# Down products of three groups one pair of Gate and Up later, cuts of w2 further apart, and a cast marked urgent

## The chip, the cores and the metric

The kernel runs on one core of a Trainium2 chip. The metric is the device time of one execution in microseconds (us). The core has TensorE (PE, matmuls), VectorE (DVE), ScalarE (ACT), GpSimd (POOL) and SyncE (SP, which issues the transfers). Each engine works through its own instructions in order and waits by semaphores for the others. Matmul results land in PSUM banks, which VectorE and ScalarE read and so set free.

## The reference

For x of 2048 tokens by 512, the kernel computes a block with windowed attention (32 heads of 16, each token sees itself and the 255 before it) that is multiplied by a gate from a SwiGLU network:

```python
xn = _layernorm(x, axis=-1)
s = _A_ref(xn, A_wqkv, A_wo)              # softmax attention in a window of 256, then @ wo
g = _silu(_B_ref(xn, B_w1, B_w3, B_w2))   # silu(silu(xn @ w1) * (xn @ w3)) @ w2, 1792 wide inside
return x + s * g
```

All inputs and the output are float32.

## The kernel before

**Precision.** Each float32 operand is held as a pair of float16 parts, a high and a low one. A product takes three matmuls: high by high, high by low and low by high. Before a weight block is cut into parts it is scaled by a factor worked out from sums of its squares. For the first tokens this is done inside the kernel: ScalarE squares the block and adds up (L249 for w1 and w3, L941 for w2), VectorE casts the sums (L261, L945), TensorE multiplies them with ones (L285), and a chain of small VectorE steps (L294 to L304, L956 to L966) makes the scale. The cut is then `split_pool` (ACT L342 and L343, POOL L345), for the first group of w2 `split` (ACT L333, DVE L334). The cut blocks are also stored in DRAM, from where the later tokens load them.

**Tiles and stages.** The tokens are worked in four tiles t of 512. The hidden width of 1792 is cut into 14 blocks f of 128 (0 to 13). For each block, `gate_up` computes Gate (12 matmuls in two halves, L1058) and then Up (12, the same line). Gate's bank is read by Tanh on ScalarE (L1073) and by a product on VectorE (L1077); Up's by a product on VectorE (L1082). A cast on ScalarE (L1091) and a subtraction on GpSimd make the pair for Down. `down(t, k, b)` (L1283) sums the blocks of group k, GROUPS = (0,4), (4,8), (8,11), (11,14), into 128 tokens b of 0 to 3, and VectorE adds each sum to an accumulator (L1304 for the first group, L1307 for the others). "Block 5" below is Gate and Up of f = 5.

**Banks.** Gate, Up, Down, `project` (Q and K, L601, read by ACT L618 and DVE L622) and the values (L567) share two banks, m0 and m1: each dense piece takes the other one, so a piece waits until the piece before the last has been read out. Scores use two buffers `s` and one `po`.

**The order.** `feed_forward` makes one list of dense pieces for the whole network. Attention is cut into units, and `spread` puts five batches of each unit (scores by column L759, masked on DVE L766 and exponentiated on ACT L769; scores by row L671, whose maxima VectorE takes at L685; values L787) between those pieces. Each piece that costs anything is a step; `later(n, f)` runs f n steps on. TensorE's instructions stay in the order in which the program writes them; those of the other engines are ordered by a scheduler by priority, and `with urgent()` gives high priority. Some of the steps, loads and measures among them, are tied to the places of the Gate and Up pieces in the list. A piece that is made early may issue its transfer, and everything that hangs on it, earlier.

`late` is what follows a pair of Gate and Up. In before, when the last block of a group has been listed, the four Down products of that group are put into `late`, and so they come after the Gate and Up of the next block: group 0 behind block 4, group 1 behind block 8, group 2 behind block 11.

Of the kernel before, what the change touches and what calls it, by code (L numbers as in the profile page):

```python
# [34 lines left out]
FB = F // P  # L35
# [48 lines left out]
def tile_block(ctx: ExitStack, tc: tile.TileContext, x, wqkv, wo, w1, w3, w2, out):  # L84
    nc = tc.nc
# [52 lines left out]
    def urgent():  # L138


        return tc.high_priority(offset=200) if started else nullcontext()
    made_so_far = [0]

    def later(n, f):
        made_so_far[0] += 1
        queue.append((now[0] + n, made_so_far[0], f))
# [776 lines left out]
    NORMS = {}  # L923
# [9 lines left out]
    def measure_down(k, f):  # L933

        f0, f1 = GROUPS[k]
        n = f1 - f0
        if f == f0:
            NORMS[k] = small.tile([P, n], F32, name="ssq2")
        sq = ppool.tile([P, D], BF16, name="sqa", bufs=1)
        with behind_exp():  # L940
            nc.scalar.activation(sq, RAW2[f], AF.Square, accum_out=NORMS[k][:, f - f0:f - f0 + 1])  # L941
        if f < f1 - 1:
            return
        sb = small.tile([P, n], BF16, name="sb2")
        nc.vector.tensor_copy(sb, NORMS[k])  # L945

        def scale(s):
            p2 = small.tile([P, n], F32, name="pp2")
            def bound():
                with tc.issue_after(lasts["emptied"].ins):  # L950
                    rest(p2)
            return then(s, powers(sb, n, p2, None, s), lambda: later(1, bound))

        def rest(p2):
            assert measured >= set(range(f0, f1))
            nc.vector.tensor_mul(p2, p2, p13[:, f0:f1])  # L956
            q = small.tile([P, 1], F32, name="q")
            nc.vector.tensor_reduce(q, p2, axis=AX.X, op=ALU.max)
            nc.vector.tensor_scalar(down_scale[:, k:k + 1], q, 1.0 / (HS * WS), None, op0=ALU.mult)
            if k:  # L960
                nc.vector.tensor_max(fold_q, fold_q, q)
            else:
                nc.vector.tensor_copy(fold_q, q)
            nc.vector.reciprocal(q, q)
            sw = small.tile([P, 4], F32, name="sw2")
            nc.vector.tensor_scalar(sw[:, 0:n], p13[:, f0:f1], q, WS, op0=ALU.mult, op1=ALU.mult)  # L966

            def cut(f):
                raw = RAW2.pop(f)
                WF.setdefault((0, f), [[None, None], None])[1] = b = take(F16)  # L970
                if k == 0:
                    with tc.issue_after(lasts["emptied"].ins):
                        split(b[:, 0:D], b[:, D:], raw, sw[:, f - f0:f - f0 + 1])
                else:
                    with behind_exp():
                        split_pool(b[:, 0:D], b[:, D:], raw, sw[:, f - f0:f - f0 + 1])
                give(raw, after=5)
            for i, f in enumerate(range(f0, f1)):
                later(1 + 2 * i, lambda f=f: cut(f))
            if f1 == FB:  # L980
                later(4, fold_scales)
        beside_scores(2, scale)
# [288 lines left out]
    def down(t, k, b):  # L1271

        f0, f1 = GROUPS[k]
        cell = {}

        def part(fs):
            if fs[0] == f0:
                cell["ps"] = bank([P, D])
            ps = cell["ps"]
            for f in fs:  # L1280
                hh, w = HH[t, f], WF[t, f][1]
                for i, (a, c) in enumerate(((0, 0), (0, 1), (1, 0))):
                    nc.tensor.matmul(ps, hh[:, a * TW + b * P:a * TW + (b + 1) * P], w[:, c * D:(c + 1) * D],  # L1283
                                     start=f == f0 and i == 0, stop=f == f1 - 1 and i == 2)
                if b == 3:
                    give(hh)
                    if t == 0:
                        def store(f=f, w=w):
                            nc.sync.dma_start(dW2[f], w)
                            give(w, after=3)  # L1290
                        later(4, store)
                    else:
                        give(w)
            if fs[-1] < f1 - 1:
                return
            if k == len(GROUPS) - 1:
                summed.add((t, b))
            if k == 0:
                ACC[t, b] = take(F32)
                with urgent():  # L1300
                    if t:
                        nc.scalar.activation(ACC[t, b], ps, AF.Copy, scale=down_scale[:, 0:1])
                    else:
                        lasts["emptied"] = nc.vector.tensor_scalar(ACC[t, b], ps, down_scale[:, 0:1], None, op0=ALU.mult)  # L1304
            else:
                with urgent():
                    lasts["emptied"] = nc.vector.scalar_tensor_tensor(ACC[t, b], ps, down_scale[:, k:k + 1], ACC[t, b],  # L1307
                                                                      op0=ALU.mult, op1=ALU.add)
        return opening([(3 * len(fs), lambda fs=fs: part(fs)) for fs in (range(f0, f0 + 2), range(f0 + 2, f1))])
# [67 lines left out]
    def feed_forward():  # L1377

        pieces = []
        late = []  # L1380
        cuts_at = []
        for t in range(NT):
            for f in range(FB):
                if t == 0:

                    if (f % 2 or f == 0) and f + LEAD < FB - 2:
                        pieces += [(0, lambda f=f: load(0, f)) for f in (range(f + LEAD, f + LEAD + 2) if f else range(4, LEAD + 1))]
                    elif f + LEAD == FB - 1:
                        pieces += [(0, lambda f=f: load(0, f)) for f in range(FB - 2, FB)]
                    if f % 2 and f + 3 < FB:  # L1390
                        pieces.append((0, lambda f=f + 3: later(8, lambda: measure(f, 1, 6)) if f == 6 else measure(f, 1)))
                    pieces += [(0, lambda f=f: load_down(0, f)) for f in range(f + 2 if f else 0, min(f + 3, FB))]
                    for m in range(f + 1 if f else 0, min(f + 2, FB)):
                        k = next(k for k, (_, f1) in enumerate(GROUPS) if m < f1)
                        pieces.append((0, lambda k=k, m=m: later(2, lambda: measure_down(k, m))))
                else:
                    if f == 0:
                        pieces += [(0, lambda t=t, f=f: load(t, f)) for f in range(2)]
                    if f + 2 < FB:
                        pieces.append((0, lambda t=t, f=f + 2: load(t, f)))  # L1400

                    if t == 1:
                        pieces.append((0, lambda t=t, f=f: load_down(t, f)))
                    if t == 1 and f in FOLD_AT:
                        work = fold_weights(FOLD_AT.index(f))
                        pieces.append((0, work[0]))
                        cuts_at.append((f + 2, work))
                    for at, work in cuts_at:
                        if t == 1 and f == at:
                            pieces.append((0, work[1]))  # L1410
                if f == FB - 4 and t + 2 < NT:
                    first, second = prepare_beside(t + 2, 8)
                    pieces += first
                if f == 0 and t > 2:
                    pieces += soon
                made = gate_up(t, f)
                for at, work in cuts_at:
                    if t == 1 and f == at:
                        made.insert(2, (0, lambda work=work: later(6, work[2])))
                pieces += made  # L1420
                pieces += late
                late = []
                if t < 2:
                    for k, (f0, f1) in enumerate(GROUPS):
                        if f == f1 - 1:
                            late = [q for b in range(4) for q in down(t, k, b)]
                for k, (j0, j1) in enumerate(FOLDS):
                    if t > 1 and f == 2 * j1 - 1:
                        soon, late = folds(t, k)
                        if k == 0 or t == NT - 1:  # L1430
                            pieces += soon
            if t + 2 < NT:
                pieces.append((0, second))
        return pieces + late
# [193 lines left out]
    for n in range(len(units)):  # L1628
        t = n // 8
# [8 lines left out]
        b = n % 8 - (2 if t < 3 else 3)  # L1638
# [6 lines left out]
    for n, u in enumerate(units):  # L1645
# [17 lines left out]
        k = n // 2 + 2  # L1663
# [35 lines left out]
```

## Time and profile before

| | |
|---|---|
| median of 3 runs | 805.73 us (805.66 to 805.86) |
| the profiled execution | 805.44 us |
| its span | 803.7 us |
| mean granted clock of TensorE | 0.999 |
| instructions in the span | 23972 |
| VectorE busy | 624.2 us (78%) |
| ScalarE busy | 393.0 us (49%) |

The span runs from the first to the last instruction that the profile shows; the execution's own time has 1.74 us more around it. In timelines the columns are start, duration, engine, source line, operation, output and inputs, shapes, the number of instructions that the row holds, and in brackets the idle time before it with what ended it. A line's number in the profile of before is one lower than in the changed kernel from L946 on, since one line was added there, and five lower from the end of `feed_forward` on. Matmuls overlap: one with 512 columns lasts 380 ns in a row, but starts come 216 ns apart in an undisturbed run of them.

### The profile page before, as it was taken

How to read it: one execution, taken by the hardware profiler on the slowest of the kernel's cores; microseconds unless marked ns; L12 is line 12 of the kernel's file. 1: busy time of each engine (PE TensorE's matmuls, PEld its weight loads, DVE VectorE, ACT ScalarE, POOL GpSimd, SP SyncE). 2: the span in 40 equal slices, each digit the busy share in tenths (PEclk: the TensorE clock that was granted, in tenths of full speed). 3: DMA queues.
4: the chain of work that ended last, by engine and by line, in shares of the span. 5: the costliest groups of instructions: out<-in, count | busy, mean ns of one | idle time of the engine just before them, and what ended most of it. 6: DMA issues, size and time to landing. Idle time of an engine off the chain costs nothing.

```text
span 803.7 us, 23972 instructions
## 1 busy us (share of the span) xinstructions
PE 791.4 (98%) x9181; PEld 404.3 (50%) x9181; DVE 624.2 (78%) x2005; ACT 393.0 (49%) x592; POOL 382.1 (48%) x746
## 2 busy tenths in 40 slices
PE   8999999999999999999999999999999999999997
PEld 4444444444554444444445444466544754466465
DVE  8887887888898678887888888777768876874537
ACT  6988685754455544345343344344444234444411
POOL 2355467552429445365443546330446276650770
PEclk9999999999999999999999999999999999999999
DMA  9887654836665564667555733665463553334431
GB/s 283 238 261 239 187 179 117 286 98 205 188 214 188 158 221 131 216 153 250 137 195 157 226 119 102 167 177 162 132 164 85 160 155 112 89 114 136 128 97 53
DMA packets 109858, 134.18 MB, mean 167 GB/s; under 512 B 18928, under 2 KB 64944, under 8 KB 109744
## 3 DMA queue, kind: packets, MB, share of 16 engines
q1 hardware_dynamic: 109456, 132.13, 55.3%
q8 instruction: 72, 1.18, 0.6%
q10 hardware_dynamic: 288, 0.52, 0.2%
q14 instruction: 42, 0.34, 0.1%
HBM read 91.23 MB, written 36.57 MB: 159 GB/s over the span
## 4 chain that ended last, share of the span: by engine, by line
PE 82%; DVE 6%; ACT 4%; DMA 3%; issue 2%; SPq 1%; POOL 0%; DVEq 0%; ACTq 0%; POOLq 0%
PE m L1058 30%; PE po L787 9%; PE m L601 9%; PE m L1283 8%; PE m L1201 7%; PE s L759 5%; PE m L1335 4%; PE m L567 4%; PE s L671 3%; PE po L671 2%; DVE junk L685 2%; ACT pt L769 1%; DMA dW<-slot 1%; ACT slot L342 1%; DVE s L766 1%
## 5 line engine op out<-in xcount | busy, mean ns | idle before, releaser
L1058 PE MATMUL m<-XH,slot 128*128 128x512 f16 x896 | 267.3, 380 | 1.2 <-DVE slot L622 0.8
L769 ACT ACTIVATE pt<-s,es 128x1024 f32<-128x1024 f32 x152 | 167.6, 1112 | 184.4 <-DVE s L766 180.4
L1058 PEld LDWEIGHTS <-slot 128*128 128x128 f16 x1344 | 125.0, 98 | 155.1 <-issue 12.5
L1058 PE MATMUL m<-XL,slot 128*128 128x512 f16 x448 | 169.8, 379 | 0.0
L766 DVE TENSOR_TENSOR s<-s,MK 128x256 f32<-128x256 f32 (+2 forms) x280 | 118.9, 435 | 53.6 <-PE s L759 48.2
L685 DVE CUSTOM_DVE_ANT_0 junk<-s,MW 128x320 bf16<-128x320 f32 x276 | 134.1, 486 | 18.7 <-PE s L671 10.6
L339 POOL TENSOR_TENSOR slot<-slot,slot 128x256 f16<-128x256 f32 (+1 forms) x86 | 57.6, 693 | 119.5 <-DVE slot L1339 54.3
L345 POOL TENSOR_TENSOR slot<-slot,slot 128x128 f16<-128x128 f32 x168 | 68.6, 442 | 73.5 <-ACT slot L343 68.2
L685 DVE CUSTOM_DVE_ANT_0 junk<-po,MW 128x320 bf16<-128x320 f32 x172 | 83.5, 486 | 5.3 <-DVE M L685 0.5
L1283 PE MATMUL m<-slot,slot 128*128 128x512 f16 x336 | 78.5, 380 | 0.3 <-DVE slot L1077 0.2
L787 PE MATMUL po<-pt,V 64*32 64x320 f32 (+4 forms) x2880 | 77.2, 342 | 0.8 <-DVE XL L525 0.8
L601 PE MATMUL m<-XH,slot 128*128 128x512 f16 x240 | 70.8, 380 | 0.4 <-DVE slot L1077 0.4
L1201 PE MATMUL m<-slot,slot 128*128 128x256 f16 x588 | 68.4, 273 | 0.1
L1073 ACT ACTIVATE slot<-m,sgs 128x512 f32<-128x512 f32 x56 | 38.3, 684 | 54.7 <-PE m L1058 54.1
L1116 POOL TENSOR_TENSOR slot<-slot,slot 128x256 f16<-128x256 f32 x98 | 64.5, 670 | 1.1
L787 PEld LDWEIGHTS po<-pt,V 64*32 64x32 f32 x2880 | 50.7, 106 | 22.6 <-PE s L515 0.9
L1201 PEld LDWEIGHTS <-slot 128*128 128x128 f16 x588 | 56.2, 98 | 11.6 <-issue 3.0
L1077 DVE SCALAR_TENSOR_TENSOR slot<-slot,m 128x512 f32<-128x512 f32 x56 | 38.3, 684 | 27.4 <-ACT slot L1073 27.4
L759 PE MATMUL s<-qa,KA 50*64 50x320 f16 (+3 forms) x1472 | 58.3, 259 | 0.1
L601 PEld LDWEIGHTS <-slot 128*128 128x128 f16 x392 | 36.5, 98 | 42.5 <-issue 1.9
L759 PEld LDWEIGHTS <-KA 50*64 50x64 f16 x1472 | 30.1, 105 | 51.9 <-issue 32.2
L1283 PEld LDWEIGHTS <-slot 128*128 128x128 f16 x336 | 30.7, 98 | 38.7 <-issue 4.3
(191 smaller groups left out, 1134.7 us busy)
## 6 DMA issues: line engine op xcount, KB each, us to landing
slot<-dW SPq DMA_DIRECT2D x98, 256.0 KB
slot<-in_B_w_dram SPq DMA_DIRECT2D x56, 256.0 KB
slot<-dFold SPq DMA_DIRECT2D x48, 256.0 KB
dW<-slot SPq DMA_DIRECT2D x42, 256.0 KB
slot<-in_A_x_dram SPq DMA_DIRECT2D x30, 256.0 KB
KA<-dK SPq DMA_DIRECT2D x24, 288.0 KB
slot<-dWQ SPq DMA_DIRECT2D x24, 256.0 KB
qa<-dQ SPq DMA_DIRECT2D x30, 192.0 KB
```

What stands on the lines that cost most here:

```text
L339: op(out[:, c], a[:, c], b[:, c])
L345: nc.gpsimd.tensor_sub(lo[:, c:c + P], raw[:, c:c + P], hi[:, c:c + P])
L601: nc.tensor.matmul(cell["pp"][:, cols[n]], w[:, (a * NC + c) * P:(a * NC + c + 1) * P], b[:, c, cols[n]], start=n == 0 and (c, i) == parts ...
L685: lasts["maximum"] = nc.vector.tensor_tensor_reduce(out=junk[:, :n], in0=s[:, r, :n], in1=mask, scale=1.0, scalar=NEG, op0=ALU.add, op1=AL ...
L759: nc.tensor.matmul(s[64 * h:64 * h + 64, r, o:o + 64 * n], ka[rows, 2 * p + a, 64 * (m + 4):64 * (m + 5)], qa[rows, 2 * p + a, 64 * (m + k ...
L766: nc.vector.tensor_add(v, v, MK[:, kind, of:of + n, :].unsqueeze(1).to_broadcast([P, 2 * len(which), n, 64]))
L769: lasts["exp"] = nc.scalar.activation(pt, s, AF.Exp, scale=es)
L787: nc.tensor.matmul(cell["po"][32 * i:32 * i + 32, h, 64 * (m + k):64 * (m + k + n)], V[64 * h:64 * h + 64, (4 * t + m // 2) % VB, hd * VW: ...
L1058: nc.tensor.matmul(cell[k], w[:, (a * NC + c) * P:(a * NC + c + 1) * P], b[:, c, :], start=c == 0 and i == 0, stop=c == NC - 1 and i == 2)
L1116: nc.gpsimd.tensor_sub(lo, view, hi)
L1201: nc.tensor.matmul(cell["ps"][:, c], made[:, f:f + P], wj[:, g:g + 256], start=j == j0 and c == 0 and n == 0, stop=j == j1 - 1 and n == 2, ...
L1283: nc.tensor.matmul(ps, hh[:, a * TW + b * P:a * TW + (b + 1) * P], w[:, c * D:(c + 1) * D], start=f == f0 and i == 0, stop=f == f1 - 1 and ...
```

## The change

Three edits. The cast of w2's summed squares is marked urgent. The cuts of w2's blocks come four steps apart instead of two, for all groups but the last. And for the first 512 tokens the Down products of groups 0 to 2 pass through a second list, `next_late`, so that they come after the Gate and Up of one more block: group 0 behind block 5, group 1 behind block 9, group 2 behind block 12. The number of instructions on each engine stays the same.

```diff
@@ measure_down
         sb = small.tile([P, n], BF16, name="sb2")
-        nc.vector.tensor_copy(sb, NORMS[k])
+        with urgent():
+            nc.vector.tensor_copy(sb, NORMS[k])
...
             for i, f in enumerate(range(f0, f1)):
-                later(1 + 2 * i, lambda f=f: cut(f))
+                later(1 + (4 if f1 < FB else 2) * i, lambda f=f: cut(f))
@@ feed_forward
-        late = []
+        late, next_late = [], []
...
                 pieces += made
                 pieces += late
-                late = []
+                late, next_late = next_late, []
                 if t < 2:
                     for k, (f0, f1) in enumerate(GROUPS):
                         if f == f1 - 1:
-                            late = [q for b in range(4) for q in down(t, k, b)]
+                            products = [q for b in range(4) for q in down(t, k, b)]
+                            if t == 0 and f1 < FB:
+                                next_late = products
+                            else:
+                                late = late + products
```

The next pieces show the order of instructions on an engine, before and after. First TensorE, where Up 4 ends (m1_1317 before, m1_1314 after is its bank). Before:

```order
L1058 LDWEIGHTS slot26_1089
L1058 MATMUL m1_1317<-XH_301,slot26_1089 128x512
L1058 LDWEIGHTS slot26_1089
L1058 MATMUL m1_1317<-XL_302,slot26_1089 128x512
L1283 LDWEIGHTS slot46_788
```

And after, at the same place:

```order
L1059 LDWEIGHTS slot26_1089
L1059 MATMUL m1_1314<-XH_301,slot26_1089 128x512
L1059 LDWEIGHTS slot26_1089
L1059 MATMUL m1_1314<-XL_302,slot26_1089 128x512
L1059 LDWEIGHTS slot17_1152
L1059 MATMUL m0_1349<-XH_301,slot17_1152 128x512
```

Gate 5 (m0_1349) stands where Down of group 0 stood. The Down products come 80 rows later, after Up 5 (m1_1415):

```order
L1059 LDWEIGHTS slot14_1188
L1059 MATMUL m1_1415<-XH_301,slot14_1188 128x512
L1059 LDWEIGHTS slot14_1188
L1059 MATMUL m1_1415<-XL_302,slot14_1188 128x512
L1284 LDWEIGHTS slot46_788
L1284 MATMUL m0_1439<-slot15_1196,slot46_788 128x512
```

Down (m0_1439) stands directly behind Up 5, in the bank that Gate 5 took.

VectorE at the same time. `po_1304` and `po_1301` are the same scores by row, slot19_1270 and slot18_1267 are Up 4's result. Before:

```order
L334 SCALAR_TENSOR_TENSOR slot45_1325<-slot51_807,sw2_1178,slot45_1325 128x512
L685 ISA junk_1302,M_1111<-s_1295,M1_106 128x256
L685 ISA M_1111 128x1
L685 ISA junk_1309,M_1111<-po_1304,MW_111 128x320
L685 ISA M_1111 128x1
L1082 SCALAR_TENSOR_TENSOR slot19_1270<-m1_1317,slot19_1270 128x512
L685 ISA junk_1311,M_1111<-po_1304,MW_111 128x320
L685 ISA M_1111 128x1
L766 TENSOR_TENSOR s_1354<-s_1354,MK_119 128x4x64
```

After:

```order
L685 ISA junk_1299,M_1111<-s_1292,M1_106 128x256
L685 ISA M_1111 128x1
L685 ISA junk_1306,M_1111<-po_1301,MW_111 128x320
L685 ISA M_1111 128x1
L685 ISA junk_1308,M_1111<-po_1301,MW_111 128x320
L685 ISA M_1111 128x1
L1083 SCALAR_TENSOR_TENSOR slot18_1267<-m1_1314,slot18_1267 128x512
L334 SCALAR_TENSOR_TENSOR slot21_1357<-slot42_711,sw2_1178,slot21_1357 128x512
L261 CAST sb_1270<-ssq_1269 128x4
L766 TENSOR_TENSOR s_1365<-s_1365,MK_119 128x4x64
```

The cut of w2 (L334) and Up's product stand behind the maxima of `po` instead of ahead of them, and a cast of sums of w1 and w3 (L261) has come in ahead of the mask addition.

ScalarE between Tanh 7 and the read-out of the project (L618, the last row of each piece). Before, thirteen instructions stand between them; these are the last eleven, and L618:

```order
L249 ACTIVATE sqa_2010,ssq_1928<-slot38_1569 128x512
L343 CAST slot24_1995<-slot8_1007 128x512
L769 ACTIVATE pt_2043<-s_2030,es1_396 128x1024
L249 ACTIVATE sqa_2020,ssq_1928<-slot0_1573 128x512
L342 ACTIVATE slot13_1107<-slot13_1107,sw2_1979 128x512
L342 ACTIVATE slot29_1103<-slot29_1103,pi_1771 128x512
L343 CAST slot4_2022<-slot13_1107 128x512
L769 ACTIVATE pt_2126<-s_2113,es1_396 128x1024
L343 CAST slot11_2071<-slot29_1103 128x512
L342 ACTIVATE slot18_1254<-slot18_1254,sw2_1979 128x512
L1091 CAST slot32_2085<-slot46_2008 128x512
L618 ACTIVATE slot34_2181<-m1_2105 128x512
```

After, Tanh 7 (L1074) and all that stands between:

```order
L1074 ACTIVATE slot25_2022<-m1_1997,sgs_155 128x512
L342 ACTIVATE slot8_1007<-slot8_1007,sw2_1993 128x512
L249 ACTIVATE sqa_2034,ssq_1949<-slot31_1342 128x512
L343 CAST slot14_2009<-slot8_1007 128x512
L769 ACTIVATE pt_2050<-s_2037,es1_396 128x1024
L342 ACTIVATE slot13_1107<-slot13_1107,sw2_1993 128x512
L1092 CAST slot3_2085<-slot25_2022 128x512
L343 CAST slot47_2087<-slot13_1107 128x512
L769 ACTIVATE pt_2128<-s_2115,es1_396 128x1024
L941 ACTIVATE sqa_2170,ssq2_2006<-slot51_1951 128x512
L249 ACTIVATE sqa_2321,ssq_2309<-slot46_2097 128x512
L618 ACTIVATE slot32_2178<-m1_2107 128x512
```

Ten instructions stand between instead of thirteen: the cuts of blocks 8 and 9 (pi_1771) are done earlier in the program, and squares of later blocks have come in.

## The prediction

> **What bounds the kernel now.** I read the page's busy times first, then the table of stretches, then TensorE's timeline in the stretches that show idle time, and last the timelines of ScalarE and VectorE at those places.
>
> The page's span and its busy times (busy, share of the span, instructions):
>
> ```profile
> span 803.7 us, 23972 instructions
> PE 791.4 (98%) x9181; PEld 404.3 (50%) x9181; DVE 624.2 (78%) x2005; ACT 393.0 (49%) x592; POOL 382.1 (48%) x746
> ```
>
> TensorE is busy for 791.4 of 803.7 us, so the time is TensorE's work plus its holes, 12.3 us. The stretches (busy time of each engine, granted clock, DMA share) show where the holes lie:
>
> ```profile
> core 0: us, PE busy (x) PEld busy (x) DVE busy (x) ACT busy (x) POOL busy (x), PEclk, DMA share, GB/s
> 60.00:100.00 40.00, 38.55 (x354) 17.62 (x352) 32.30 (x118) 29.93 (x56) 18.63 (x43) 1.00 0.69 213
> 100.00:140.00 40.00, 36.99 (x528) 19.04 (x527) 32.80 (x124) 28.26 (x53) 28.14 (x72) 1.00 0.47 147
> 140.00:200.00 60.00, 60.00 (x646) 28.18 (x644) 51.26 (x188) 35.06 (x56) 25.31 (x65) 1.00 0.61 194
> 200.00:760.00 560.00, 559.08 (x6943) 287.50 (x6942) 432.61 (x1336) 243.70 (x319) 270.47 (x473) 1.00 0.54 159
> ```
>
> The order changes only between about 70 us (the end of Up 4) and about 200 us; before and after that TensorE has the same instructions in the same order. In this stretch it idles 1.45 + 3.01 = 4.46 us, all of it before 140 us. From 140 to 760 us there is 0.92 us of idle time. So a gain or loss made before 140 us is carried to the end whole: nothing behind it waits long enough to swallow it. The most that the change can win is about 4.4 us.
>
> The instructions are the same in number and kind in both kernels, so every term is a wait that grows or goes. I compare the start of a fixed TensorE instruction in before with where it must come after. Each hole is named by the row behind it; the brackets hold the idle time and its releaser.
>
> **At block 5.** TensorE's rows where Down of group 0 now stands (start, duration, instruction):
>
> ```profile
> 70.69 1.46 PE L1283 MATMUL m<-slot,slot 128*128 128x512 f16 x6 [0.25 <-DVE slot L1077]
> 72.24 0.42 PE L759 MATMUL s<-qa,KA 50*64 50x320 f16 x10
> 73.08 0.33 PE L671 MATMUL s<-KA,qa 48*64 48x320 f16 x4 [0.43 <-ACT pt L769]
> 73.89 0.33 PE L671 MATMUL po<-KA,qa 48*64 48x320 f16 x4 [0.47 <-DVE M L685]
> 74.15 5.35 PE L1283 MATMUL m<-slot,slot 128*128 128x512 f16 x24
> 79.44 0.33 PE L671 MATMUL s<-KA,qa 48*64 48x320 f16 x4
> 79.60 0.18 PE L285 MATMUL s<-sb,onesb 64*64 64x4 bf16 x4
> ```
>
> ScalarE, VectorE and GpSimd there, from their own timelines:
>
> ```profile
> 69.22 0.70 ACT L1073 ACTIVATE slot<-m,sgs 128x512 f32<-128x512 f32 x1
> 76.19 1.09 ACT L769 ACTIVATE pt<-s,es 128x1024 f32<-128x1024 f32 x1
> 69.94 0.69 DVE L1077 SCALAR_TENSOR_TENSOR slot<-slot,m 128x512 f32<-128x512 f32 x1 [0.41 <-ACT slot L1073]
> 71.09 0.75 DVE L334 SCALAR_TENSOR_TENSOR slot<-slot,sw,slot 128x512 f16<-128x512 f32 x1
> 66.05 1.94 POOL L345 TENSOR_TENSOR slot<-slot,slot 128x128 f16<-128x128 f32 x4 [0.17 <-ACT slot L343]
> ```
>
> In the row at 70.69 Down starts right behind Up 4 and waits until Gate 4's bank is emptied: Tanh at 69.22, product at 69.94, free at 70.63. After the change Gate 5 stands in that place and takes the same bank, so this wait stays. The exponential for which 73.08 waits has the same instructions ahead of it in both orders: no change. The wait of 73.89 is for the maxima that empty `po`. One cut of w2 (L334, 0.75 us) and the Up product (L1082) stand ahead of them on VectorE. After the change the cut comes later and the maxima stand ahead of both, so this wait goes: 73.89 comes right behind 73.08, as 0.16 us lie between the rows 79.44 and 79.60. I take 0.65 us of gain for the 0.81 between 73.08 and 73.89.
>
> What is new is the wait behind it. Gate 5 then ends at 74.8 and Up 5 (12 matmuls at 5.35 / 24 = 0.22 us each, from the row of 74.15: 2.6 us) at 77.4. Down's first matmul needs Gate 5's bank. Tanh 5 stands on ScalarE right behind the exponential that runs from 76.19 to 77.2 in before. So: Tanh 77.2, product 0.72 later (69.22 to 69.94) at 77.9, bank free 0.69 later, at 78.6. TensorE waits from 77.4 to 78.65, 1.25 us. The sum at the row of 79.44 is −0.65 + 1.25 = **+0.60**. The bounds of that hole: about 0 if the exponential in front of Tanh 5 runs a whole length (1.09) earlier than in before, and 2.3 (1.25 + 1.09) if it runs as much later. I keep 1.25: on ScalarE the instructions ahead of that exponential are of the same kinds as in before, and its row is there.
>
> The weights of block 5 don't hold Gate 5 back: the last of their cuts on GpSimd ends at 68.0 (66.05 + 1.94), 2.7 us ahead.
>
> **From 87 to 101 us.** TensorE again, and the cast that the urgent mark moves:
>
> ```profile
> 87.79 0.30 PE L671 MATMUL po<-KA,qa 48*64 48x256 f16 x4
> 88.02 0.61 PE L1058 MATMUL m<-XH,slot 128*128 128x512 f16 x2
> 95.73 0.31 PE L671 MATMUL po<-KA,qa 48*64 48x320 f16 x4
> 96.24 0.59 PE L1058 MATMUL m<-XH,slot 128*128 128x512 f16 x2 [0.20 <-DVE slot L622]
> 100.22 0.33 PE L671 MATMUL s<-KA,qa 48*64 48x320 f16 x4
> 100.88 0.20 PE L285 MATMUL s<-sb,onesb 64*64 64x4 bf16 x4 [0.33 <-DVE sb L945]
> 100.66 0.17 DVE L945 CAST sb<-ssq 128x4 bf16<-128x4 f32 x1
> ```
>
> At 96.24 Gate 6 waits for the project's bank (L622). After the change the project stands further ahead and Down's bank, emptied by one VectorE instruction, is taken: 95.73 to 96.24 is 0.51, the same step without a wait (87.79 to 88.02) 0.23, so **−0.28**. At 100.88 the product with ones waits for the cast of the sums, which VectorE does at 100.66 although the sums were long complete. In before the cast stands on VectorE directly ahead of the product of Gate 6, after the change ten instructions stand between them: 0.66 between 100.22 and 100.88, 0.16 without a wait, so **−0.50**. By 101 us the net is −0.18, say −0.2.
>
> **From 105 to 126 us.** TensorE, then ScalarE:
>
> ```profile
> 111.23 0.59 PE L601 MATMUL m<-XH,slot 128*128 128x512 f16 x2 [0.43 <-DVE slot L1077]
> 113.76 0.30 PE L671 MATMUL s<-KA,qa 48*64 48x256 f16 x4 [0.73 <-ACT pt L769]
> 119.98 0.59 PE L1058 MATMUL m<-XH,slot 128*128 128x512 f16 x2 [0.43 <-DVE slot L622]
> 122.35 0.38 PE L1058 MATMUL m<-XL,slot 128*128 128x512 f16 x1
> 122.81 1.46 PE L1283 MATMUL m<-slot,slot 128*128 128x512 f16 x6
> 124.48 0.33 PE L671 MATMUL s<-KA,qa 48*64 48x320 f16 x4 [0.22 <-DVE al L295]
> 125.83 1.58 PE L787 MATMUL po<-pt,V 64*32 64x320 f32 x49 [0.79 <-DVE XL L525]
> 109.78 0.67 ACT L1073 ACTIVATE slot<-m,sgs 128x512 f32<-128x512 f32 x1
> 110.35 0.61 ACT L343 CAST slot<-slot 128x512 f16<-128x512 f32 x1
> 112.60 1.11 ACT L769 ACTIVATE pt<-s,es 128x1024 f32<-128x1024 f32 x1
> 118.60 0.60 ACT L618 ACTIVATE slot<-m 128x512 f16<-128x512 f32 x1
> 121.34 0.69 ACT L1073 ACTIVATE slot<-m,sgs 128x512 f32<-128x512 f32 x1
> ```
>
> At 111.23 the project waits for Gate 7's bank. Tanh 7 (109.78) stands behind the same number of instructions in both kernels, and ScalarE is not late because of TensorE there; TensorE arriving 0.2 earlier waits 0.2 longer. The net returns to **0**, with ±0.2.
>
> Then ScalarE's queue is shorter, since the cuts of blocks 8 and 9 were done earlier. Between Tanh 7 and the exponential at 112.60 stand three instructions instead of four; one cast takes 110.35 to 110.86, some 0.5 us. So the hole of 0.73 at 113.76 shrinks by at most 0.5; I take **−0.40**. Between Tanh 7 and the project's L618 (118.60) stand ten instead of thirteen, so L618 may run 1.5 us earlier; the wait of 0.43 at 119.98 goes, with the gap in the pipeline 0.84 to 0.36: **−0.48**. Tanh 8 (121.34) follows earlier, and with it the bank that 122.81 waits for: 0.46 from 122.35, against one interval of 0.22, is **−0.24**. On VectorE the mask add, the steps of the scale chain (L295) and the split of the transposed scores (L525) stand behind the product of Gate 8. With that product earlier the step to 124.48 loses its idle 0.22 and a little of the pipeline's fill: **−0.28**; of the idle 0.79 at 125.83 I take half, **−0.42**, since the transposition in front still has to be done.
>
> **The sum.** 0 + (−0.40 − 0.48 − 0.24 − 0.28 − 0.42) = **−1.8 us**. After 126 us Gate 9 and Up 9 stand where the second group's Down stood. Scores and values lie between Gate 9 and the moved Down, and a project between Gate 12 and the third group's Down, so Tanh has over 3.5 us there, and I count nothing. The profiled execution took 805.44 us, its span 803.7; the sum gives a span of 801.9, an execution of 803.6. It lies 0.29 under the median of 805.73, so the median becomes **803.9 us**. A measurement of this kernel can tell about 0.2% from no change, 1.6 us, so the forecast is just beyond it.
>
> **Rivals.** *The later gains don't come (wash), 805.4 us.* ScalarE's queue is shorter, but if score blocks arrive as late as before (the mask adds on VectorE set the exponential), L618 and Tanh 8 stay where they are. Then 0 to −0.4 is left, 805.3 to 805.7. For it: VectorE is busy 32.80 of 40 us in 100 to 140. Against it: the rows at 113.76 and 119.98 wait on ScalarE's instructions. Chance 0.27.
>
> *No hole at block 5, 802.6 us.* If ScalarE does Tanh 5 early enough, the hole of 1.25 is gone, and TensorE keeps that lead if Tanh 7 comes earlier with it; −1.8 − 1.25 = −3.1. Chance 0.09.
>
> *The bank wait takes over (slower), 807.9 us.* Down's first matmul comes right behind Up, and at block 5 only Up's 2.6 us covers Tanh and product, at block 9 Up and the scores before it, 3.6 (72.24 to 73.08 and the four products behind, 0.84 + 0.16). If the product ends more than 4.9 us behind its Gate's last matmul (the forecast has 3.8), the hole at block 5 is 2.3, and at block 9 it is 1.3. The sum: −0.65 + 2.3 − 0.28 − 0.50 + 1.3 = +2.2, provided that the later start of everything on TensorE also delays VectorE's and ScalarE's chain, so that 111 us resets nothing and the gains of 113 to 126 are void. It decides from the one exponential more or less that stands ahead of Tanh 5. Chance 0.15.
>
> *The clock drops.* More short waits at banks could let the clock fall. Two rows of short stretches at the start show its price:
>
> ```profile
> 1.00:4.00 3.00, 2.96 (x8) 1.07 (x9) 1.83 (x4) 2.34 (x2) 2.96 (x15) 1.00 0.65 227
> 4.00:8.00 4.00, 3.80 (x18) 1.64 (x17) 3.47 (x12) 2.74 (x4) 1.30 (x4) 1.00 1.08 329
> ```
>
> In the first, matmuls come 0.375 us apart (3.00 / 8), in the second 0.222 (4.00 / 18). A slow stretch of 3 us costs 3.00 − 8 × 0.222 = 1.2 us; two of them, one at block 5 and one at block 9, take 2.4 from the 1.8 gained: +0.6, 806.3 us. Against it: the longest hole in before, 0.79, slowed nothing behind it, and the row at 74.15 with 24 matmuls holds full pace straight after two holes. Chance 0.02. The Trainium skill ("TensorE: Matmul & The Clock Gate", section "A second HAM failure mode: psum-queue depth-cycling") states that a kernel which cycles through PSUM banks can idle so briefly and often that the clock gate swings between half and full, and that the cost lies in the re-warming and not in the single matmul. That rule speaks against this change, which adds such a wait; the row at 74.15 does not agree with it here.
>
> That the change does nothing isn't a rival: the order shows the moves.
>
> **How the numbers follow.** The forecast has 0.47, spread over 802.9 to 804.9: of it I put 0.39 beyond −0.2% and 0.08 within. The wash gives 0.24 within and 0.03 faster, the case without a hole 0.09 faster, the bank wait 0.15 slower, the clock 0.02 within, since 806.3 is inside 0.2%. Faster 0.39 + 0.03 + 0.09 = 0.51, same 0.08 + 0.24 + 0.02 = 0.34, slower 0.15. The range reaches down to 802.4, past most of the case without a hole, and up to 806.8, past the wash and short of the bank wait's 807.9: some 0.04 below and 0.16 above are left out.
>
> **What would show it right or wrong.** In the profile of the changed kernel, Down's first matmul behind Up 5 has an idle of about 1.1 us released by the product; the product with ones of w2's sums has none by the cast; the projects' and Gates' rows between 113 and 126 have 1.8 us less idle in sum; from 140 us on there is none. It is wrong if a hole of over 0.5 us stands at block 9 or 12, if idle between 100 and 140 stays at 3.0, or if matmuls of 128x512 come more than 0.22 us apart anywhere behind 8 us.

## The result and the profile after

The changed kernel takes 803.86 us (median of 15 runs, 803.48 to 804.58), the kernel before 805.73 us in the same comparison. The ratio is 0.9979, with a 95% interval of 0.9971 to 0.9986: 1.9 us or 0.21% faster, between 0.14% and 0.29%. One of the 15 executions of before took 826.34 us and is not in the ratio. The forecast was 803.9 us.

The table of stretches of the changed kernel (busy time of each engine, granted clock, DMA share); its span is 801.8 us:

```profile
60.00:100.00 40.00, 38.06 (x354) 17.26 (x352) 33.08 (x124) 34.19 (x66) 23.25 (x55) 1.00 0.69 217
100.00:140.00 40.00, 39.12 (x517) 19.62 (x516) 35.57 (x136) 29.84 (x55) 25.79 (x66) 1.00 0.53 164
140.00:200.00 60.00, 59.69 (x665) 28.41 (x663) 49.20 (x177) 32.98 (x50) 27.38 (x73) 1.00 0.58 188
```

TensorE's idle time from 60 to 100 us grew from 1.45 to 1.94 us, from 100 to 140 it fell from 3.01 to 0.88, and from 140 to 200 it is 0.31 where there was none. ScalarE is busy for 34.19 instead of 29.93 us in the first stretch and for 29.84 instead of 28.26 in the second: work of both stretches has moved forward, and squares of later blocks have come into the second. The clock is 1.00 in all of them, so that rival did not come.

TensorE's timeline at the places of the prediction (start, duration, instruction, and in brackets the idle time with its releaser), in the changed kernel:

```profile
70.69 0.59 PE L1059 MATMUL m<-XH,slot 128*128 128x512 f16 x2 [0.25 <-DVE slot L1078]
73.09 0.33 PE L671 MATMUL s<-KA,qa 48*64 48x320 f16 x4 [0.60 <-ACT pt L769]
73.22 0.33 PE L671 MATMUL po<-KA,qa 48*64 48x320 f16 x4
78.64 1.46 PE L1284 MATMUL m<-slot,slot 128*128 128x512 f16 x6 [1.09 <-DVE slot L1078]
80.02 0.33 PE L671 MATMUL s<-KA,qa 48*64 48x320 f16 x4
96.53 0.60 PE L1059 MATMUL m<-XH,slot 128*128 128x512 f16 x2
100.68 0.18 PE L285 MATMUL s<-sb,onesb 64*64 64x4 bf16 x4
111.04 0.59 PE L601 MATMUL m<-XH,slot 128*128 128x512 f16 x2 [0.47 <-DVE slot L1078]
113.12 0.30 PE L671 MATMUL s<-KA,qa 48*64 48x256 f16 x4 [0.28 <-ACT pt L769]
118.68 0.33 PE L671 MATMUL po<-KA,qa 48*64 48x320 f16 x4
119.18 0.60 PE L1059 MATMUL m<-XH,slot 128*128 128x512 f16 x2
121.78 0.59 PE L1059 MATMUL m<-XH,slot 128*128 128x512 f16 x2
123.17 0.33 PE L671 MATMUL s<-KA,qa 48*64 48x320 f16 x4
123.66 2.06 PE L787 MATMUL po<-pt,V 64*32 64x320 f32 x72
146.40 0.59 PE L1059 MATMUL m<-XH,slot 128*128 128x512 f16 x2 [0.19 <-DVE slot L1308]
```

And ScalarE and VectorE around Tanh 5, the project's read-out and Tanh 8:

```profile
76.19 1.09 ACT L769 ACTIVATE pt<-s,es 128x1024 f32<-128x1024 f32 x1
77.19 0.68 ACT L1074 ACTIVATE slot<-m,sgs 128x512 f32<-128x512 f32 x1
117.00 0.58 ACT L618 ACTIVATE slot<-m 128x512 f16<-128x512 f32 x1
118.79 0.68 ACT L1074 ACTIVATE slot<-m,sgs 128x512 f32<-128x512 f32 x1
77.90 0.69 DVE L1078 SCALAR_TENSOR_TENSOR slot<-slot,m 128x512 f32<-128x512 f32 x1 [0.78 <-ACT slot L1074]
```

The reader sees the chain at block 5 as it was worked out: exponential 76.19, Tanh 77.19, product 77.90, Down at 78.64. The read-out of the project (L618) runs at 117.00 instead of 118.60, Tanh 8 at 118.79 instead of 121.34. Of the ten rows with a marked wait that the prediction showed between 70 and 126 us, three start where they did or nearly so and still wait (70.69, 73.09, 111.04), one has a shorter wait (113.12), the other six waits are gone; 78.64 and 146.40 are new. At 118.68 and at 188.57 no wait is marked, but there are small ones of 0.13 and 0.12 us, of which more below.

Start against start (the changed kernel less before, at the same instruction or the same place in the order), with the forecast beside it:

| row in before | forecast, sum so far | measured |
|---|---|---|
| 79.44, scores behind Down or Up | +0.60 | +0.58 |
| 96.24, Gate 6 | +0.32 | +0.29 |
| 100.88, product with ones | −0.18 | −0.20 |
| 111.23, project | 0 ± 0.2 | −0.19 |
| 113.76, scores by row | −0.40 | −0.64 |
| 119.98, Up 8 | −0.88 | −0.80 |
| 122.81, Down before, Gate 9 after | −1.12 | −1.03 |
| 124.48, scores by row | −1.40 | −1.31 |
| 125.83, values | −1.82 | −2.17 |
| end of the span | −1.8 | −1.9 |

### The profile page after: what moved, and what is told of

Same layout as the page of the kernel before. It is cut to its first block, busy times and chain, and to the rows that moved or that the text cites. A ratio compares the mean times of both kernels' runs of the same rounds, so it can differ in the third digit from the quotient of the medians.

```text
span 801.8 us, 23974 instructions
## 1 busy us (share of the span) xinstructions
PE 791.1 (99%) x9181; PEld 403.8 (50%) x9181; DVE 623.0 (78%) x2005; ACT 393.9 (49%) x592; POOL 381.2 (48%) x746
## 4 chain that ended last, share of the span: by engine, by line
PE 80%; DVE 8%; DMA 4%; ACT 3%; issue 2%; POOL 1%; SPq 1%; DVEq 0%; ACTq 0%; POOLq 0%
PE m L1059 31%; PE po L787 9%; PE m L601 8%; PE m L1202 8%; PE m L1284 7%; PE s L759 5%; PE m L1336 4%; PE m L567 4%; PE s L671 3%; DMA slot<-in_B_w_dram 2%; DVE junk L685 2%; PE po L671 2%; ACT sqa L249 1%; DVE s L766 1%; POOL slot L345 1%
## 5 line engine op out<-in xcount | busy, mean ns | idle before, releaser
L787 PE MATMUL po<-pt,V 64*32 64x320 f32 (+4 forms) x2880 | 77.2, 342 | 0.1
L1074 ACT ACTIVATE slot<-m,sgs 128x512 f32<-128x512 f32 x56 | 38.3, 684 | 59.8 <-PE m L1059 59.7
```

Of the source, the lines that this page charges most:

```text
L787: nc.tensor.matmul(cell["po"][32 * i:32 * i + 32, h, 64 * (m + k):64 * (m + k + n)], V[64 * h:64 * h + 64, (4 * t + m // 2) % VB, hd * VW: ...
```

## Experiments

The start of the row at block 5 (70.69 in both kernels) differs between profiled executions by up to 0.6 us, although the instructions ahead of it are the same. So starts are compared less that start. The first table column is the median with that of before in the same comparison; "project" is the row of 111 us, "scores" that of 113 us, "last" the start of the last matmul of the execution.

| kernel | median, before | start at block 5 | project | scores | last |
|---|---|---|---|---|---|
| before | 805.73 | 70.69 | 40.54 | 43.07 | 728.8 |
| changed | 803.86, 805.73 | 70.69 | 40.35 | 42.43 | 727.0 |
| e1, cast alone | 805.93, 805.81 | 70.91 | 40.61 | 43.15 | 729.1 |
| e2, delay alone | 804.99, 805.81 | 70.85 | 40.35 | 43.06 | 728.7 |
| e3, no cast | 804.50, 805.81 | 71.23 | 40.39 | 42.48 | 727.3 |
| e4, no spacing | 805.13, 805.81 | 71.16 | 40.37 | 43.08 | 728.1 |
| e5, group 0 | 803.11, 805.85 | 70.85 | 40.36 | 42.45 | 726.0 |
| e6, groups 1 and 2 | 806.35, 805.85 | 71.08 | 40.61 | 43.15 | 729.3 |
| e7, larger hole | 804.89, 805.85 | 71.04 | 40.87 | 42.96 | 727.6 |
| e8, rstd early | 804.48, 805.85 | 70.64 | 40.68 | 42.77 | 728.4 |
| e9, smaller hole | 803.03, 805.99 | 71.22 | 39.95 | 42.03 | 725.6 |
| e10, groups 0 and 1 | 804.31, 805.99 | 71.27 | 40.36 | 42.46 | 726.7 |
| e11, group 0, no cast | 803.41, 805.99 | 70.75 | 40.36 | 42.45 | 726.1 |

The profiled execution of e2 took 805.63 us, 0.6 above its median, with a wait of 0.53 at 522 us in it, so its last column is late. The traces of e2, e4 and e7 each have a wait of about 0.25 us at 710 to 711 us, and no other trace has it; their last column holds it too. The intervals of the ratios are some 1.5 us wide, and most of the changed kernels differ by less, so what separates two of them is read from the traces.

### e1: the cast alone

```diff
 # kernel before
-        nc.vector.tensor_copy(sb, NORMS[k])
+        with urgent():
+            nc.vector.tensor_copy(sb, NORMS[k])
```

> The kernel before with the urgent cast alone. Theory A (the cuts' place on ScalarE decides): the wait of 0.5 us at the product with ones goes, but the exponential at 107.5 us hangs on the layernorm chain on GpSimd, which starts no earlier, so nothing is carried on: 805.7 us, within 0.2 of before. Theory B (every removed wait is carried to the end): 805.2 us.

The ratio is 1.0002 (0.9993 to 1.0011): nothing. And the reason is simpler than either theory. TensorE's row of the product with ones in e1:

```profile
101.03 0.20 PE L285 MATMUL s<-sb,onesb 64*64 64x4 bf16 x4 [0.26 <-DVE sb L946]
```

The wait is still there, 0.26 instead of 0.33. Here the mark alone moves the cast only one instruction forward on VectorE. The instruction that it passes (L448) is the one that starts GpSimd's layernorm steps, and the project comes 40.61 − 40.54 = 0.07 us later, although the product with ones came 0.07 earlier.

### e3 and e11: without the urgent mark

```diff
 # e3: changed kernel; e11: with group 0 alone delayed (e5)
-        with urgent():
-            nc.vector.tensor_copy(sb, NORMS[k])
+        nc.vector.tensor_copy(sb, NORMS[k])
```

> The changed kernel without the urgent mark on the cast. Theory A: ScalarE's order is that of the changed kernel, the lost 0.5 us at the product with ones is swallowed at 111 us: 803.9 us. Theory B: it is carried: 804.4 us.

> Group 0 alone delayed, without the urgent mark on the cast. If the mark helps only at the wait of 147 us, which group 0 alone does not have: 803.1 us, as with the mark. If it helps elsewhere too: 803.4 us or slower.

In e3 and in e11 the product with ones near 100 us has no wait on the cast either, and project and scores come where they come with the mark. In e2, which has neither mark nor spacing, that wait is gone too. So the delay took it away, not the mark. What the mark does in the changed kernel comes later; TensorE's row of Gate 10 in e3:

```profile
147.35 0.59 PE L1058 MATMUL m<-XH,slot 128*128 128x512 f16 x2 [0.56 <-DVE slot L1307]
```

The wait is 0.56 us with the plain cast and 0.19 with the urgent one (146.40 above), a difference of 0.37; the last matmul comes 0.3 later. The ratio to before is 0.9983 (0.9974 to 0.9992). The gain on before is 1.31 us by the medians instead of 1.87. The intervals overlap, so that the mark is worth something is shown by the traces, where it is 0.3 us at the end. For e11, 803.41 against 803.11 of e5 is within what the two can tell, and the last matmul lies 0.1 apart.

### e2 and e4: without the wider spacing

```diff
 # e2: also without the urgent mark; e4: with it
-                later(1 + (4 if f1 < FB else 2) * i, lambda f=f: cut(f))
+                later(1 + 2 * i, lambda f=f: cut(f))
```

> The kernel before with the delayed Down products alone: no urgent cast, cuts of w2 two steps apart. Theory A: most of the gain, less what the cuts of w2 cost that come back between Tanh 7 and the project's read-out (twelve instructions instead of ten, four instead of three ahead of the exponential): about -1.0 us, 804.7 us. Rival: spacing and cast carry half of the gain or more: 805.2 us or slower.

> The changed kernel with the cuts of w2 two steps apart again. Theory A: as the delay alone, 804.7 us, because ScalarE has two instructions more between Tanh 7 and the project's read-out. Rival: spacing does nothing: 803.9 us.

Ratios 0.999 (0.9981 to 0.9999) and 0.9991 (0.9983 to 1.0): 0.8 and 0.7 us of gain. By the medians the spacing is worth 0.5 us beside the delay without the mark (1.31 in e3 less 0.82 in e2) and 1.2 with it (1.87 less 0.68 in e4); the intervals do not tell these two apart, nor do they decide whether delay alone brings less than half of the gain. In neither e2 nor e4 does Gate 10 wait, so there the mark has nothing to take. TensorE in e4:

```profile
74.36 0.33 PE L671 MATMUL po<-KA,qa 48*64 48x320 f16 x4 [0.47 <-DVE M L685]
79.11 1.45 PE L1284 MATMUL m<-slot,slot 128*128 128x512 f16 x6 [0.43 <-DVE slot L1078]
114.24 0.30 PE L671 MATMUL s<-KA,qa 48*64 48x256 f16 x4 [0.90 <-ACT pt L769]
120.17 0.33 PE L671 MATMUL po<-KA,qa 48*64 48x320 f16 x4 [0.55 <-DVE XL L525]
```

Two things are to be seen. With the old spacing the wait for the maxima (74.36) is back, and Down's wait (79.11) is shorter by as much: Down starts 79.11 − 71.16 = 7.95 us after the start at block 5, as in the changed kernel (78.64 − 70.69 = 7.95). The moved cuts gain nothing at block 5, because Down waits for the product anyway. What they gain comes at 113 us: 43.08 − 42.43 = 0.65 us, the wait for the exponential, which has one more cut ahead of it on ScalarE. The row that waits for the split of the transposed tokens (L525) adds 0.37: it starts 120.17 − 71.16 = 49.01 us behind block 5 instead of 118.68 − 70.69 = 47.99, 1.02 later in all. At Gate 10, where e4 has no wait, it gets back 0.35.

### e5, e6 and e10: which group

```diff
 # e5: k == 0; e6: k in (1, 2); e10: k < 2
-                            if t == 0 and f1 < FB:
+                            if t == 0 and k == 0:
 # e6 alone, so that the cuts of an undelayed group 0 are in time
-                later(1 + (4 if f1 < FB else 2) * i, lambda f=f: cut(f))
+                later(1 + (4 if k in (1, 2) else 2) * i, lambda f=f: cut(f))
```

> The changed kernel with only group 0 delayed (groups 1 and 2 behind blocks 8 and 11 as before). Theory A: the gain comes from group 0 alone, since its delay brings the cuts of blocks 8 and 9 forward (eight instructions between Tanh 7 and the project's read-out instead of thirteen): 803.6 to 804.0 us. Rival: groups 1 and 2 matter: 804.6 us or slower.

> The changed kernel with only groups 1 and 2 delayed, group 0 behind block 4 and its cuts two steps apart as before. Theory A: thirteen instructions stand between Tanh 7 and the read-out as before, so the waits from 113 us on stay: 805.5 us, within 0.4 of before. Rival: 804.6 us or faster.

> The changed kernel with groups 0 and 1 delayed and group 2 behind block 11 as before. If what groups 1 and 2 cost against group 0 alone (0.8 us) comes at the bank of Down of group 1 (the waits at 118.7 and 146.4 in the changed kernel, 0.13 and 0.19 idle): 803.5 us, nearer to group 0 alone (803.1) than the changed kernel with a rest of 0.3 for group 2. If group 2 makes all of it: 803.1 us; if group 1 does: 803.9 us.

Group 0 alone gives more than the change: 803.11 us, ratio 0.9966 (0.9953 to 0.9978), an interval that still touches that of the change; in the traces it is 1.0 us. Groups 1 and 2 alone give 1.0007 (0.9998 to 1.0016), no gain. Groups 0 and 1 give 0.998 (0.9971 to 0.9989), by the median slower than all three forecasts of it and not to be told from the changed kernel. In the traces the last matmul comes at 726.0, with group 1 delayed too 726.7, with group 2 also 727.0: group 1's delay costs 0.7 us and group 2's 0.2. The first piece has TensorE's waits in e5 from 100 to 200 us, these two and no others; the second has the scores of 113 us and Gate 10 in e6, the third Gate 10 in e10:

```profile
111.21 0.59 PE L601 MATMUL m<-XH,slot 128*128 128x512 f16 x2 [0.47 <-DVE slot L1078]
113.30 0.30 PE L671 MATMUL s<-KA,qa 48*64 48x256 f16 x4 [0.29 <-ACT pt L769]
```

```profile
114.23 0.30 PE L671 MATMUL s<-KA,qa 48*64 48x256 f16 x4 [0.73 <-ACT pt L769]
149.13 0.59 PE L1059 MATMUL m<-XH,slot 128*128 128x512 f16 x2 [0.60 <-DVE slot L1308]
```

```profile
147.00 0.59 PE L1059 MATMUL m<-XH,slot 128*128 128x512 f16 x2 [0.19 <-DVE slot L1308]
```

With group 1 delayed, Gate 10 stands behind Down of group 1 and waits until VectorE has added Down's sum (L1308). Start against start, nearly all of the 0.7 us is found in two places: e10 lags e5 by 0.30 us from the scores into `po` on (118.57 in e5, 119.29 in e10) and by 0.66 from this row of Gate 10 on (145.92, 147.00). The idle times there are smaller, 0.14 and 0.19, since they do not count the gaps in the pipeline. Group 2's 0.2 stands behind the values at 188.57: from there on the changed kernel lags e10 by 0.20 (192.60 and 192.98).

How many instructions ScalarE has between Tanh 7 and L618 differs between the kernels, and TensorE follows (starts less the start at block 5; "values" is the row of 125.83 us in before, 123.66 in the changed kernel):

| instructions between | kernels | L618 | values |
|---|---|---|---|
| 13 | before, e1 | 47.91, 47.99 | 55.14, 55.22 |
| 13 | e6 | 48.00 | 54.87 |
| 12 | e2, e4 | 47.31, 47.32 | 53.97, 53.99 |
| 10 | changed, e3, e10 | 46.31, 46.35, 46.33 | 52.97, 53.02, 52.99 |
| 8 | e5, e11 | 44.95, 44.95 | 52.69, 52.69 |

No run changes this count alone: spacing, groups and the order on VectorE change with it.

### e7 and e9: the hole at block 5 larger and smaller

```diff
 # e7, changed kernel: the exponential behind Gate 5's first half comes behind Tanh 5
+            def exponential():
+                with urgent(), behind_exp():
+                    lasts["exp"] = nc.scalar.activation(pt, s, AF.Exp, scale=es)
+            if swap.pop("at", None):      # set by gate_up(0, 5)
+                later(2, exponential)
+            else:
...
 # e9, on e5: the squares of blocks 8 and 9 one step later
-  ... if f == 6 else measure(f, 1)))
+  ... if f == 6 else later(1, lambda: measure(f, 1, 6)) if f == 8 else measure(f, 1)))
```

> The changed kernel with the exponential behind Gate 5 put behind Tanh 5 on ScalarE; two squares come ahead of Tanh 5 in its place, so Tanh 5 runs some 0.6 us later and the wait of Down behind Up 5 grows from 1.1 to 1.7 us. As the prediction has it (111 us resets what came before): 803.9 us. Rival (the delay of TensorE delays VectorE's layernorm steps and is carried to the end): 804.5 us.

> Group 0 alone delayed, and the squares of blocks 8 and 9 one step later, so that two squares that stood ahead of the exponential in front of Tanh 5 stand behind Tanh 5; everything later keeps its order. The exponential can then start when its mask is added (75.54 in the changed kernel) instead of at 76.19, and the wait of Down behind Up 5 shrinks from 1.09 to about 0.45 us. If a wait before 100 us is carried on (as the larger hole showed): 0.65 us less than with group 0 alone, 802.5 us. As the prediction has it (111 us resets it): 803.1 us.

TensorE in e7, then ScalarE and TensorE in e9:

```profile
79.50 1.46 PE L1293 MATMUL m<-slot,slot 128*128 128x512 f16 x6 [1.60 <-DVE slot L1087]
111.91 0.59 PE L601 MATMUL m<-XH,slot 128*128 128x512 f16 x2 [0.48 <-DVE slot L1087]
```

```profile
76.17 1.11 ACT L769 ACTIVATE pt<-s,es 128x1024 f32<-128x1024 f32 x1 [0.73 <-DVE s L766]
78.64 1.46 PE L1284 MATMUL m<-slot,slot 128*128 128x512 f16 x6 [0.56 <-DVE slot L1078]
```

The larger hole (1.60 instead of 1.09) comes out at the project as 40.87 − 40.35 = 0.52 us, with the project's own wait unchanged at 0.48: nothing is swallowed there. The median is 804.89, ratio 0.9992 (0.9983 to 1.0001). The smaller hole (0.56) comes out as 40.36 − 39.95 = 0.41, and 0.4 at the last matmul, against e5. Its exponential now starts 0.10 us behind the end of its mask addition (75.78 + 0.29 = 76.07 on VectorE), which the expectation left out, so the hole shrank by 0.53 and not by 0.65. The median, 803.03 with a ratio of 0.9963 (0.9951 to 0.9976), is the lowest of all kernels here, but it lies only 0.08 under e5, with a start at block 5 that was 0.37 later in its trace. That it is faster than e5 is shown by the trace, not by the times.

### e8: the layernorm's steps earlier

```diff
-        work.append(lambda: rstd(0, 4))
+        if t == 1:
+            last = work.pop()
+            work += [lambda: (last(), rstd(0, 4)), lambda: None]
+        else:
+            work.append(lambda: rstd(0, 4))
```

> The changed kernel with the three VectorE steps ahead of the second tile's layernorm chain on GpSimd one batch of scores earlier; the centring stays where it is. If that chain sets the exponential at 107 us and with it Tanh 7: VectorE's wait of 0.45 us for it goes, and the project at 111.04 comes 0.4 to 0.5 us earlier, 803.4 us. Rival (VectorE or TensorE set them): 803.9 us.

GpSimd's last step of that chain, VectorE's read of it, and TensorE's values and project in e8, with two waits that come later:

```profile
102.63 0.20 POOL L474 TENSOR_TENSOR rs<-sq,r 128x4 f32<-128x4 f32 x1
103.45 0.78 DVE L477 TENSOR_SCALAR slot<-slot,mv,rs 128x512 f32<-128x512 f32 x1
101.12 2.05 PE L791 MATMUL po<-pt,V 64*32 64x320 f32 x72 [0.31 <-DVE M L689]
111.32 0.59 PE L605 MATMUL m<-XH,slot 128*128 128x512 f16 x2 [0.42 <-DVE slot L1082]
142.34 0.33 PE L675 MATMUL po<-KA,qa 48*64 48x320 f16 x4 [0.21 <-DVE XL L525]
147.50 0.59 PE L1063 MATMUL m<-XH,slot 128*128 128x512 f16 x2 [0.60 <-DVE slot L1312]
```

The chain was done earlier and VectorE no longer waited for it (no bracket at 103.45), and still the project came 40.68 − 40.35 = 0.33 us later. Two of the three small steps now stand ahead of the project's split on VectorE and all three ahead of the maxima of `po`; the values at 101.12 wait for those maxima. So the second tile's layernorm on GpSimd does not by itself set the place of the project; VectorE's queue ahead of the maxima does as well. The last matmul comes 1.4 us later than in the changed kernel (in an execution that took 0.55 more than e8's median): 0.33 is there from the project on, the rest comes mainly at the last two rows, of which the first waits in e8 only and the second waits 0.60 instead of 0.19, although the cast is urgent here. The median is 804.48, ratio 0.9985 (0.9976 to 0.9993). Both theories missed: neither expected it later.

## Why the prediction was right, point by point

**What bounds the kernel** held: the gain is idle time of TensorE, taken from the stretch of 100 to 140 us, and it came to the end nearly whole.

**Block 5, +0.60** was measured as +0.58, with Tanh at 77.19 where 77.2 was worked out and Down at 78.64 where 78.65 was. But its two parts are not two terms. e4 shows that the −0.65 at the maxima changes nothing when Down waits behind it for Tanh. The term is the place of Down alone.

**Gate 6, −0.28**, was −0.29. **The product with ones, −0.50**, was −0.49, but the cause given was wrong: the urgent mark alone left 0.26 of 0.33 us of that wait (e1), and without the mark the wait is gone as well (e2, e3, e11). The mark's own gain in the changed kernel is at 147 us, some 0.3 to 0.4, at a wait that the prediction did not have.

**111 us, back to 0**, is the step that failed: it measured −0.19, and what is won or lost at block 5 is not reset there. A loss of 0.5 came through as 0.52 (e7) and a gain of 0.5 as 0.41 (e9). The prediction held that ScalarE is not late because of TensorE there, but in the changed kernel Tanh 7 hangs on TensorE by a longer way. VectorE waits for TensorE's scores of 88 us to add the mask, and from there on it has no idle time above 0.15 us until the three small steps that start the layernorm on GpSimd (L443 to L448, done at 100.43). Ten steps of GpSimd follow, VectorE waits for the last of them, and the exponential ahead of Tanh 7 waits for a mask that VectorE adds behind that:

```profile
88.55 0.43 DVE L766 TENSOR_TENSOR s<-s,MK 128x256 f32<-128x256 f32 x1 [0.85 <-PE s L759]
103.32 0.63 DVE L477 TENSOR_SCALAR slot<-slot,mv,rs 128x512 f32<-128x512 f32 x1 [0.45 <-POOL rs L474]
107.21 1.11 ACT L769 ACTIVATE pt<-s,es 128x1024 f32<-128x1024 f32 x1 [0.19 <-DVE s L766]
```

What TensorE wins at 96 and 101 us comes behind the place where this chain leaves it, and a lead won there alone (0.07 in e1) was not carried. So that its lead was 0.20 at 101 us and 0.19 at the project is a coincidence. The mask above is 0.60 us later than in before (87.95), as block 5 has it; by the last small step VectorE is 0.33 ahead (100.26, in before 100.59), since its instructions between stand in another order and two waits of before on ScalarE (0.28 us at 91.51, 0.20 at 95.50) are gone. The bounds of ±0.2 covered the 0.19 without this having been seen.

**113 us, −0.40**, was −0.64 + 0.19 = −0.45, and e2 and e4 show the cause: with one more cut ahead of the exponential the wait is 0.90. **Up 8, −0.48**, was −0.16. L618 ran 1.60 us earlier and the wait of 0.43 went, as said, but the scores into `po` at 118.68 came 0.31 us behind the row at 118.37, since they wait for VectorE's L525. In before L525 stood ahead of L622 on VectorE, in the changed kernel it stands behind it, and L622 waits for L618. TensorE's and VectorE's rows in the changed kernel, and then two rows of TensorE in before, where the scores came 0.03 behind:

```profile
118.37 0.18 PE L285 MATMUL s<-sb,onesb 64*64 64x4 bf16 x4
117.61 0.69 DVE L622 SCALAR_TENSOR_TENSOR slot<-m,slot 128x512 f16<-128x512 f32 x1 [0.57 <-ACT slot L618]
118.22 0.41 DVE L525 TENSOR_TENSOR XL<-po,XH 128x256 f16<-128x256 f32 x1
```

```profile
118.97 0.18 PE L285 MATMUL s<-sb,onesb 64*64 64x4 bf16 x4
119.00 0.31 PE L671 MATMUL po<-KA,qa 48*64 48x320 f16 x4
```

e5, with eight instructions ahead of L618 and not ten, has no such wait. **122.81, −0.24**, was −0.23, and **124.48, −0.28**, was −0.28. **125.83, −0.42**, was −0.86: the wait of 0.79 went whole and not by half.

**After 126 us nothing** was not right either: from −2.17 the lead fell to −1.81 at Gate 10 (146.40, in before 148.21) and to −1.60 behind the values at 188.57 (192.60, in before 194.20); behind 200 us small differences brought it to −1.9. The mis-sized terms at 111 us (−0.19 where 0 was said), at 119.98 (0.32 too much) and at 125.83 (0.44 too little) and this 0.3 nearly cancel. That the sum came out within 0.1 us of the measured one is luck; the single terms were off by up to 0.44.

**The rivals.** The wash did not come: ScalarE did L618 and Tanh 8 earlier. The bank wait behind Tanh came once, as forecast, and not at blocks 9 or 12; what the later groups' delay costs stands elsewhere, at the scores behind L525, at Down's bank ahead of Gate 10 and at the values of 188.57. The case without a hole did not come, but e9 shows that what is taken from the hole does reach the end. The clock stayed at 1.00: six matmuls behind the hole of 1.09 us (78.64) and behind that of 1.60 in e7 (79.50) take 1.46 us, as at 70.69 in before. The prediction's case for this rival had two wrong readings, which changed no term: the longest idle times of before are not 0.79 but two of 1.04 us, at 1.04 and 8.84 us, and the granted clock of its row with matmuls 0.375 us apart is 1.00, so that row does not show what a lower clock costs.

**The signs** that the prediction named came but for one: Down behind Up 5 idles 1.09 us, the product with ones has no wait, the waits of the rows from 113 to 126 us fell by 1.8, from 2.17 to 0.41 us, and blocks 9 and 12 have no hole. From 140 us on there was to be no idle time; there are 0.31 us of it up to 200.

## What to carry to other kernels

When a piece is moved ahead of others, what hangs on its place (here loads, squares and cuts of weights on ScalarE) moves too, and may be worth more than the piece: of three delayed groups only the first helped, and the traces put most of its gain down to ScalarE's cuts, which came forward with it. Count the instructions between two waits on the engine that is waited for; that gave single holes to 0.05 us (78.64 for 78.65), and missed by 0.3 to 0.4 where VectorE's order had changed as well (119.98, 125.83). Before saying that a later wait swallows an earlier gain, ask what the releaser itself waits for: if it hangs on the gaining engine by a longer way, the gain goes through.

## What was not expected

A priority mark on one instruction moved it one place and changed nothing by itself (e1), and gained 0.3 to 0.4 us at another place 46 us later when the order around it had changed (146.40 against 147.35). And freeing an engine from a wait of 0.45 us did not bring the project forward but put it back by 0.33 (e8). The three steps that did it stand in a queue that others wait for: 0.84 and 0.17 us for the two below, and 0.25 for the third (L448 at 99.72). By the medians e8 is 1.37 us under its before and the changed kernel 1.87, but their intervals overlap.

```profile
96.73 0.84 DVE L443 TENSOR_SCALAR ve<-mv 128x4 f32<-128x4 f32 x1
97.61 0.17 DVE L447 TENSOR_SCALAR r<-ve 128x4 int32<-128x4 int32 x1
```
